# Loading q, k and the weights by GpSimd transfers that cast to f16, with a new order of all steps

## The chip, the cores and the metric

The kernel runs on one core of a Trainium2 chip. Its engines work side by side, each through its own queue in order: TensorE (PE, matmuls; PEld is its weight load), VectorE (DVE), ScalarE (ACT), GpSimd (POOL) and SyncE (SP), which here only issues transfers. 16 DMA engines move the data between HBM and SBUF. The metric is the device time of one launch in microseconds.

## The reference

Sliding-window causal attention (8 batches, 8 heads, 576 positions, head size 64, window 64), and then a gated MLP with a spatial matmul over the positions:

```
scores = q k^T / 8, kept where 0 <= row - column < 64
x      = softmax(scores) v                        # heads side by side: (8, 576, 512)
h      = relu(x @ w_in);  u, v = h[:512], h[512:] # w_in 512 x 1024
v_n    = (v - mean) / sqrt(var + 1e-6)            # over the 512 columns
v_s    = w_spatial @ v_n + b_spatial              # w_spatial 576 x 576
out    = (u * v_s) @ w_out                        # w_out 512 x 512
```

All inputs and the output are float32; the matmuls are in float16.

## The kernel before

The program is a list of small steps. Functions add them to a plan, each with what it computes, the buffers that it takes and uses, and the steps that it depends on. A text at the head of the file, `ORDER`, then gives the order of all steps as words `name:engine:buffers`. The steps are emitted in exactly this order, so it fixes the queue of every engine. Nothing else schedules the program; an instruction waits only where data or a buffer is not ready. `PH` marks a PE step whose matmuls are split into two halves of 64 output rows.

For each batch b and each half g of its heads (four heads) there are these steps:

- `ldk`, `ldq`, `ldv`: loads by SP. k and q come as one transfer of 128 x 1152 f32 each (576 KB) into a staging buffer `nat`, of which there are eight; v comes in five pieces into `natv`. `ldwin`, `ldwsp`, `ldwo`, `ldb` load the weights and the bias through the same `nat` buffers.
- `ck`, `cq`, `cwin`, `cwsp`, `cwo`, `cb`: casts from `nat` to f16, on the engine that `ORDER` names. Those of k and q go into `hqk` (four buffers). `cv` casts v into `hv`; `sl`, `su` and `s4` copy it, shifted by 64 rows, into `hs`.
- `tk`, `tq`: DVE transposes k and q in blocks of 32 x 32, into `qkT`.
- `S` (scores on PE), `E` (exponential on ACT), `M` (the mask, a minimum on DVE), `Z` (row sums on PE), `N` and `n` (the inverse through logarithm and exponential on ACT), `P` (product with v on PE), `X` (multiply by the inverse on DVE). `S_r`, `E_r` and so on do the last 64 rows, for one batch or for a pair of batches.

For each batch follow `V` (the v half of x @ w_in), `Vr` (relu), `Vb` and `Va` (statistics), `L1` and `L2` (the inverse deviation), `A` (normalise), `U` and `Ur` (the u half), `G` (spatial matmul), `Ge` (the gate), `O` (w_out), `Oe` (copy out) and `st` (store). `W` transposes w_spatial on PE, with `We` as its copies. So V of batch 0 needs all X of batch 0 and half of w_in (`ldwin1*`); G of batch 0 needs all A of batch 0 and w_spatial; U needs the other half of w_in.

`D` are dummy matmuls on zeroed scratch data, placed among the first steps; they keep PE busy while it has no data.

The lines that the prediction's rows name: L292, L295, L298, L300 are the copy or cast on ACT, on POOL (k and q in three pieces), on POOL (v) and on any other; L412 and L433 issue the loads of k, q and v; L419 transposes; L479 is S, L489 M, L502 Z, L514 P, L522 X, L606 X_r; L614 and L617 are the whole and the halved matmuls of V, U, G and O; L671 Vb, L728 A, L862 D.

Of the kernel before, what the change touches and what calls it, by code (L numbers as in the profile page):

```python
# [18 lines left out]
D24:PE:0 ldb:DQ:0 D5:PE:1 D21:PE:2 ldk0_0:DQ:1 ck0_0:DVE:0 tk0_0:DVE:0 D18:PE:3 D2:PE:2 D14:PE:2  # L19
D19:PE:3 D10:PE:0 ldq0_0:DQ:2 ldk0_1:DQ:3 ldv0_00:DQ:0 ldq0_1:DQ:4 ldv0_10:DQ:1 D3:PE:3 ldv0_11:DQ  # L20
cv0_10:POOL:0 ldk1_0:DQ:5 ck0_1:ACT:1 ldv0_12:DQ ldv0_13:DQ ldv0_01:DQ cq0_0:DVE:2 ldq1_0:DQ:6
tq0_0:DVE:1 ldv0_02:DQ D1:PE:2 S0_0:PE:0:1 tk0_1:DVE:2 D22:PE:0 E0_01:ACT:0 E0_00:ACT:1 cq0_1:DVE:3
tq0_1:DVE:3 D15:PE:3 D6:PE:1 D0:PE:2 D26:PE:0 D23:PE:3 S0_r:PE:1:0 E0_r0:ACT:0 E0_r1:ACT cv0_11:POOL
sl0_10:DVE:0 M0_00:DVE ldv0_03:DQ su0_10:DVE M0_01:DVE ck1_0:DVE:0 M0_r:DVE D8:PE:1 Z0_00:PE:2
ldv0_04:DQ ldwin110:DQ:7 ldv0_14:DQ ldwin111:DQ ldwin100:DQ:1 S0_1:PE:1:0 N0_00:ACT:0 E0_11:ACT:2
D16:PE:0 D7:PE:3 E0_10:ACT:3 M0_11:DVE Z0_01:PE:1 Z0_r:PE:2 D4:PE:0 Z0_11:PE:3 N0_r:ACT:1
N0_01:ACT:2 cv0_00:ACT:1 N0_11:ACT:3 ldwin101:DQ su0_11:DVE M0_10:DVE D12:PE:0 Z0_10:PE:2 D20:PE:1
sl0_11:POOL tk1_0:DVE:4 sl0_00:ACT:1 N0_10:ACT:4 n0_11:ACT n0_10:ACT cq1_0:POOL:2 tq1_0:DVE:5
ldq1_1:DQ:2 ldk1_1:DQ:3 P0_10:PE:0 P0_11:PE:3 cwin110:ACT n0_01:ACT D11:PE:1 cv0_01:POOL
ldwin000:DQ:4 ldwin010:DQ:5 ldwin001:DQ ldwin011:DQ ldwsp1:DQ:6 X0_10:DVE:0 su0_00:DVE X0_11:DVE  # L30
n0_00:ACT sl0_01:POOL cb:POOL su0_01:POOL S1_0:PE:0:1 D25:PE:2 D13:PE:1 P0_00:PE:0 X0_00:DVE:1
E1_01:ACT:3 s40_1:ACT P0_01:PE:2 D9:PE:3 cwin111:POOL cwin100:POOL cwin101:POOL ck1_1:POOL:1
s40_0:ACT E1_00:ACT:2 cwin010:POOL X0_01:DVE cwin001:POOL cwin011:POOL V0_2:PE:1 M1_01:DVE
Vr0_2:ACT:0 n0_r:ACT P0_r:PE:3 Z1_01:PE:0 V0_0:PE:2 ldwsp3:DQ:0 M1_00:DVE N1_01:ACT:5 Vr0_0:ACT:1
cq1_1:DVE:3 Z1_00:PE:1 V0_3:PH:0 V0_1:PE:2 N1_00:ACT:4 cwin000:ACT Vr0_3:ACT:2 Vr0_1:ACT:3
ldwsp0:DQ:7 ldwsp4:DQ:1 ldwsp2:DQ:2 cwsp1:POOL:6 ldv1_00:DQ:2 ldq2_0:DQ:3 X0_r:DVE:0 tq1_1:DVE:7
Vb0_2:DVE:0 V0_4:PE:3 tk1_1:DVE:8 S1_1:PE:1:0 cwsp3:POOL:0 cwsp0:POOL:1 Vb0_0:DVE:1 Vb0_3:DVE:2
Vr0_4:ACT:4 Va0_3:DVE Vb0_4:DVE:3 Va0_4:DVE Va0_0:DVE Va0_2:DVE Vb0_1:DVE:4 Va0_1:DVE U0_2:PH:1
U0_3:PH:0 ldk2_0:DQ:4 U0_4:PE:2 ldv1_01:DQ ldv1_02:DQ ldv1_03:DQ E1_11:ACT:1 E1_10:ACT:0 cwsp2:POOL
cq2_0:POOL:0 M1_10:DVE ldv1_10:DQ:3 Ur0_2:ACT:0 L10:ACT:0 ldv1_11:DQ ldv1_12:DQ ldv1_13:DQ L20:ACT  # L40
ldv1_14:DQ ldq2_1:DQ:5 ldv1_04:DQ ldk2_1:DQ:6 ldwo00:DQ:0 ldwo01:DQ Ur0_4:ACT:1 S1_r:PE:0:1
Z1_10:PE:3 U0_0:PE:1 ldwo10:DQ:7 ldwo11:DQ U0_1:PE:2 E1_r0:ACT:0 Ur0_3:ACT:2 E1_r1:ACT Ur0_0:ACT:3
# [158 lines left out]
def kernel(  # L201
# [11 lines left out]
    nc = tc.nc  # L213
# [88 lines left out]
    def cost(n, a=True, d=True, p=True, d1=False):  # L302
# [613 lines left out]
```

## Time and profile before

| | |
|---|---|
| time, median of 3 runs | 196.34 us (195.63 to 197.69) |
| profiled execution, first to last instruction | 193.6 us; its own time with what lies around it is not in the profile |
| PE busy | 184.9 us (95%), 3218 matmuls, dummies included |
| DVE, ACT, POOL busy | 163.7 (85%), 157.1 (81%), 87.4 us (45%) |
| DMA moved | 42.73 MB, mean 221 GB/s |
| q and k loads, median to landing | 6.1 and 6.6 us for 576 KB |

PE's busy time counts a matmul up to its modelled end, so a PE that reads as full need not be at its peak, and dummy matmuls count as work. Waits are put down to what ended last. Rows of the timeline give start, duration, engine, line, operation, tiles and count, and in brackets the idle time before them with its releaser.

### The profile page before, as it was taken

The numbers are of one execution on the slowest core, as the hardware profiler recorded it, in microseconds if no ns is written. First come the engines' busy times: TensorE is split into PE (matmuls) and PEld (weight loads), VectorE is DVE, ScalarE is ACT, GpSimd is POOL, SyncE is SP. The second block draws the span as 40 slices with busy tenths as digits, with TensorE's granted clock in tenths as the row PEclk, the third lists the DMA queues.
The fourth block names the chain that finished last, engine by engine and source line by source line (L and its number), as shares of the span: only waits on it lengthen the run. The fifth ranks groups of instructions, "written<-read, shape, count | busy, mean of one in ns | idle before, by whom it ended". The sixth has DMA issues, their size and how long they took to land.

```text
span 193.6 us, 7606 instructions
## 1 busy us (share of the span) xinstructions
PE 184.9 (95%) x3218; PEld 107.0 (55%) x3218; DVE 163.7 (85%) x304; ACT 157.1 (81%) x282; POOL 87.4 (45%) x161
## 2 busy tenths in 40 slices
PE   7798998999999999999999999999999999999991
PEld 2352534556556664656665656565756565665560
DVE  4899899999999999998999999998996967468331
ACT  2269998998999999899979999999999875706430
POOL 4027775849932986701956577615641520000000
PEclk9999999999999999999999999999999999999999
DMA  5999999899989997619987999669958000600445
GB/s 177 373 316 290 391 355 333 168 275 373 242 205 332 261 335 179 149 38 289 367 230 184 310 310 282 196 177 218 306 125 266 22 3 0 224 30 0 135 166 191
DMA packets 50421, 42.73 MB, mean 221 GB/s; under 512 B 39377, under 2 KB 39761, under 8 KB 50386
## 3 DMA queue, kind: packets, MB, share of 16 engines
q1 hardware_dynamic: 50162, 42.04, 73.3%
q8 instruction: 25, 0.41, 0.9%
q10 hardware_dynamic: 224, 0.20, 0.3%
q14 instruction: 10, 0.08, 0.1%
HBM read 32.79 MB, written 9.44 MB: 218 GB/s over the span
## 4 chain that ended last, share of the span: by engine, by line
PE 70%; DVE 13%; ACT 9%; DMA 3%; issue 2%; SPq 1%
PE bank L617 50%; PE bank L614 4%; PE pair L479 4%; PE bank L514 3%; DMA nk<-in_k_dram 3%; PE bank L502 3%; ACT e L486 3%; DVE qT L419 2%; PE bank L702 2%; DVE e L489 2%; DVE kT L419 2%; DVE st L671 2%; DVE g L797 1%; DVE x L522 1%; ACT lz L529 1%
## 5 line engine op out<-in xcount | busy, mean ns | idle before, releaser
L617 PE MATMUL bank<-wspT,vn 128*64 128x512 f16 (+3 forms) x530 | 39.1, 296 | 0.0
L486 ACT ACTIVATE e<-pair 128x1024 f16<-128x1024 f32 x32 | 32.0, 1030 | 1.6 <-PE pair L479 1.4
L797 DVE TENSOR_TENSOR g<-bank,ru 128x512 f16<-128x512 f32 (+1 forms) x36 | 23.3, 654 | 9.4 <-PE bank L617 7.0
L647 ACT COPY ob<-bank 128x512 f32<-128x512 f32 (+1 forms) x38 | 21.9, 591 | 9.7 <-PE bank L617 8.4
L669 ACT ACTIVATE vs<-bank 128x512 f16<-128x512 f32 (+1 forms) x40 | 23.8, 602 | 7.1 <-PE bank L705 5.6
L617 PE MATMUL bank<-x,win 128*64 128x512 f16 (+2 forms) x304 | 29.1, 327 | 0.0
L617 PEld LDWEIGHTS <-vn 128*64 128x64 f16 (+1 forms) x530 | 20.8, 111 | 13.2 <-issue 0.2
L671 DVE BATCH_NORM_STATS2 st<-vs 128x6 f32<-128x512 f16 (+1 forms) x40 | 26.0, 670 | 2.3 <-ACT vs L669 2.2
L298 POOL COPY hs<-hv 64x512 f16<-64x512 f16 (+1 forms) x36 | 20.1, 585 | 16.3 <-ACT hv L292 8.4
L617 PE MATMUL bank<-win,x 128*64 128x512 f16 x216 | 27.0, 379 | 0.0
L617 PE MATMUL bank<-wout,g 128*64 128x512 f16 (+1 forms) x208 | 24.7, 371 | 0.0
L522 DVE TENSOR_TENSOR x<-bank,lz 128x512 f16<-128x512 f32 x32 | 21.2, 684 | 3.5 <-PE bank L514 2.2
L489 DVE TENSOR_TENSOR e<-e,mask 128x1024 f16<-128x1024 f16 x32 | 23.0, 725 | 0.5 <-ACT e L486 0.4
L763 ACT ACTIVATE ru<-bank 128x512 f32<-128x512 f32 (+1 forms) x38 | 21.6, 584 | 1.5 <-PE bank L617 0.8
L295 POOL CAST hk<-nk 128x384 f16<-128x384 f32 x36 | 19.4, 574 | 7.1 <-DMA nk<-in_k_dram 6.7
L529 ACT ACTIVATE lz<-bank 128x512 f32<-128x512 f32 x32 | 19.0, 599 | 1.9 <-PE bank L502 1.6
L298 POOL CAST hv<-nv 128x512 f16<-128x512 f32 x18 | 11.7, 661 | 18.8 <-DMA nv<-in_v_dram 18.7
L419 DVE STREAM_TRANSPOSE kT<-hk 128x576 f32<-128x576 f32 x16 | 19.9, 1241 | 0.2 <-ACT hk L292 0.2
L419 DVE STREAM_TRANSPOSE qT<-hq 128x576 f32<-128x576 f32 x16 | 19.8, 1237 | 0.2
L531 ACT ACTIVATE lz<-lz 128x512 f32<-128x512 f32 x32 | 19.6, 642 | 0.0
L295 POOL CAST hq<-nq 128x384 f16<-128x384 f32 x27 | 14.9, 588 | 10.3 <-DMA nq<-in_q_dram 7.8
L617 PEld LDWEIGHTS <-win 128*64 128x64 f16 x304 | 14.4, 110 | 9.2
(91 smaller groups left out, 298.9 us busy)
## 6 DMA issues: line engine op xcount, KB each, us to landing
nk<-in_k_dram SPq DMA_DIRECT2D x16, 576.0 KB, 6.6
nq<-in_q_dram SPq DMA_DIRECT2D x16, 576.0 KB, 6.1
nv<-in_v_dram SPq DMA_DIRECT2D x64, 128.0 KB, 5.9
out_dram<-ob SPq DMA_DIRECT2D x14, 512.0 KB, 5.8
wi<-in_moe_w_in_dram SPq DMA_DIRECT2D x8, 256.0 KB, 5.8
ws<-in_moe_w_spatial_dram SPq DMA_DIRECT2D x4, 288.0 KB, 7.6
nv<-in_v_dram SPq DMA_DIRECT2D x16, 64.0 KB, 4.5
wo<-in_moe_w_out_dram SPq DMA_DIRECT2D x4, 256.0 KB, 7.2
```

The source lines that it names most:

```text
L295: nc.gpsimd.tensor_copy(o[:, n:n + 384], i[:, n:n + 384])
L298: nc.gpsimd.tensor_copy(o[:, lo:hi, :, :], i[:, lo:hi, :, :])
L419: d = add(f"t{name}{b}_{g}", ("DVE", 1.09), key, lambda e: nc.vector.transpose(qt.t[:, :].rearrange("p (i j) -> p j i", j=18), h.t[:, :].b ...
L486: ex = add(f"E{b}_{g}{u}", ("ACT", 0.91), key, lambda e, u=u: nc.scalar.activation(e2[u].t[:, :, :], sc[u].t[:, :, :], AF.Exp, bias=0.0, s ...
L489: mins.append(add(f"M{b}_{g}{u}", ("DVE", 0.65), key, lambda e, u=u: nc.vector.tensor_tensor(e2[u].t[:, :, :], e2[u].t[:, :, :], mask[:, : ...
L522: lambda e, u=u, ob=ob, lz=lz: nc.vector.tensor_tensor(x.t[:, u, :], ob.t[:, :], lz.t[:, :], ALU.mult),
L617: nc.tensor.matmul(o[c:c + 64, :], w[:, c:c + 64], x, start=start, stop=stop)
L647: lambda e: (nc.vector.tensor_copy if last else nc.scalar.copy)(view(), m.t[rows, 0:n]),
L669: rl = add(f"Vr{b}_{j}", ("ACT", 0.49), key, lambda e: nc.scalar.activation(vs.t[0:jn, :], m.t[0:jn, :], AF.Relu), deps=[pv], acq=[vs], us ...
L671: s1 = add(f"Vb{b}_{j}", ("DVE", 0.6), key + 0.02, lambda e: nc.vector.bn_stats(st6.t[0:jn, 0:6], vs.t[0:jn, :]), deps=[rl], acq=[st6], us ...
L763: lambda e, m=m, ru=ru, n=n: nc.scalar.activation(ru.t[:, 0:n], m.t[:, 0:n], AF.Relu), deps=[pu], acq=[ru], uses=[m])))
L797: nc.vector.tensor_tensor(g.t[:, 0:n], m.t[:, 0:n], ru.t[:, 0:n], ALU.mult)
```

## The change

All transfers of q, k, w_in, w_spatial, w_out and the bias are issued by POOL instead of SP, with an f16 destination, so that they cast on the way. The cast steps `ck`, `cq`, `cwin`, `cwsp`, `cwo` and `cb` and the `nat` buffers go. `hqk` has eight buffers instead of four. Each half of w_in is one transfer, w_out is one, and w_spatial two. The loads of v and the stores stay on SP. The identity for PE's transposes and the two rows of ones move from the start of POOL's queue to a step `consts`. A step `A` may run on POOL, and 22 of the 40 do. A small step `hold` on ACT makes the loads of v of batch 0, half 0, wait for the first k load; it stands behind the first exponential. The dummies are 12 pairs and 31 single matmuls of 512 columns instead of 25 pairs and 18 of 128. `ORDER` is new throughout; of it the first lines before and after stand here.

```diff
 ORDER = """
-D24:PE:0 ldb:DQ:0 D5:PE:1 D21:PE:2 ldk0_0:DQ:1 ck0_0:DVE:0 tk0_0:DVE:0 D18:PE:3 D2:PE:2 D14:PE:2
+D0:PE:0 D1:PE:1 D2:PE:2 D3:PE:3 D4:PE:0 D5:PE:1 D6:PE:2 D7:PE:3 D8:PE:0 D9:PE:1 D10:PE:2 D11:PE:3
+ldv0_10:DQ:0 ldq0_0:POOL:0 tq0_0:DVE:0 ldk0_0:POOL:1 tk0_0:DVE:1 S0_0:PE:0:1 E0_01:ACT:0
...
-NWARM, NFILL, FILL = 27, 2, 9
-BUFS = {"nat": 8, "natv": 4, "hqk": 4, "qkT": 9, ...
+NWARM, NFILL, FILL = 43, 31, 1
+HOLD_AT, HOLD_FOR = 1, (0, 0)
+BUFS = {"natv": 4, "hqk": 8, "qkT": 9, ...
...
-    make_identity(nc, id16[:])
...
-        nc.gpsimd.memset(vn4_t[i][64:65, :], 1.0)
...
+    def emit_consts(e):
+        make_identity(nc, id16[:])
+        for i in range(NSB):
+            nc.gpsimd.memset(vn4_t[i][64:65, :], 1.0)
+    add("consts", ("POOL", 1.8), -2.0, emit_consts)
...
+            ld = add(f"ldwin{half}", ("POOL", 0.85), key + 0.01 * (1 - half),
+                     lambda e, cs=cs: nc.gpsimd.dma_start(
+                         w_in_all[:, :, cs], moe_w_in[:, cs].rearrange("(r p) f -> p r f", r=4)))
...
+        nat = [
+            add("ldwsp0", ("POOL", 0.85), key, lambda e: nc.gpsimd.dma_start(
+                wsp_nat[:, 0:4, :], moe_w_spatial[0:512, :].rearrange("(t p) s -> p t s", t=4))),
+            add("ldwsp4", ("POOL", 0.55), key + 0.001, lambda e: nc.gpsimd.dma_start(
+                wsp_nat[0:64, 4, :], moe_w_spatial[512:576, :]))]
...
-            n = buf("nat", f"n{name}{b}_{g}")
-            ld = add(f"ld{name}{b}_{g}", ("DQ", 0.45), key, lambda e: nc.sync.dma_start(
-                n.t[:, :], src[b, 4 * g:4 * g + 4, :, :].rearrange("h (i j) d -> (h i) (j d)", j=18)),
-                acq=[n], nbytes=1.57, n=128)
             h = buf("hqk", f"h{name}{b}_{g}")
-            c = add(f"c{name}{b}_{g}", cost(1152), key,
-                    lambda e: cp(e, h.t[:, :], n.t[:, :]), deps=[ld], acq=[h], uses=[n])
+            ld = add(f"ld{name}{b}_{g}", ("POOL", 0.55), key, lambda e: nc.gpsimd.dma_start(
+                h.t[:, :], src[b, 4 * g:4 * g + 4, :, :].rearrange("h (i j) d -> (h i) (j d)", j=18)),
+                acq=[h])
...
+        if (b, g) == HOLD_FOR:
+            held, hld = HELD[-1]
+            lds.append(add("hold", ("ACT", 0.1), key, lambda e: nc.scalar.copy(
+                nv.t[0:1, 0, 0, 0:1], held.t[0:1, 0:1]), deps=[hld], acq=[nv], uses=[held]))
...
-            AP.append(add(f"A{b}_{j}", ("DVE", 0.33), key + 0.2, emit_A,
+            AP.append(add(f"A{b}_{j}", [("DVE", 0.33), ("POOL", 0.6)], key + 0.2, emit_A,
```

The start of POOL's queue before, from the end of `keep` on (the first digits in a name are batch and half; the last number only counts):

```order
L247 AFFINE_SELECT keep_79<-keep_79 128x64
masks.py:197 MEMSET id16_83 128x128
masks.py:199 AFFINE_SELECT id16_83<-id16_83 128x128
L264 MEMSET vn4_0_98 1x512
L264 MEMSET vn4_1_99 1x512
L300 CAST hv0_1_154<-nv0_1_149 128x512 x2
L300 COPY hs0_1_279<-hv0_1_154 64x512
L295 CAST hq1_0_408<-nq1_0_165 128x384 x3
L300 CAST hv0_0_385<-nv0_0_145 128x512
```

The same place now:

```order
L243 AFFINE_SELECT keep_79<-keep_79 128x64
L367 DMA hq0_0_132<-in_q_dram 128x1152
L367 DMA hk0_0_136<-in_k_dram 128x1152
L367 DMA hk0_1_199<-in_k_dram 128x1152
L367 DMA hq0_1_207<-in_q_dram 128x1152
L367 DMA hk1_0_309<-in_k_dram 128x1152
L367 DMA hq1_0_315<-in_q_dram 128x1152
L294 COPY hs0_1_350<-hv0_1_242 64x256
L367 DMA hk1_1_439<-in_k_dram 128x1152
L367 DMA hq1_1_509<-in_q_dram 128x1152
L322 DMA win_98<-in_moe_w_in_dram 128x4x512
L329 DMA wspn_100<-in_moe_w_spatial_dram 128x4x576
```

Six loads go out ahead of the first copy, which waits for a cast of v; the rest of the first loads stand behind it.

DVE before, from the first cast on to the transpose of the fourth load:

```order
L300 CAST hk0_0_127<-nk0_0_125 128x1152
L419 STREAM_TRANSPOSE kT0_0_129<-hk0_0_127 128x18x32
L300 CAST hq0_0_163<-nq0_0_141 128x1152
L419 STREAM_TRANSPOSE qT0_0_167<-hq0_0_163 128x18x32
L419 STREAM_TRANSPOSE kT0_1_229<-hk0_1_158 128x18x32
L300 CAST hq0_1_237<-nq0_1_147 128x1152
L419 STREAM_TRANSPOSE qT0_1_239<-hq0_1_237 128x18x32
```

The same place now, up to the first cast of v:

```order
L373 STREAM_TRANSPOSE qT0_0_134<-hq0_0_132 128x18x32
L373 STREAM_TRANSPOSE kT0_0_138<-hk0_0_136 128x18x32
L373 STREAM_TRANSPOSE kT0_1_201<-hk0_1_199 128x18x32
L373 STREAM_TRANSPOSE qT0_1_209<-hq0_1_207 128x18x32
L447 TENSOR_TENSOR e2_0_01_197<-e2_0_01_197,mask_84 128x1024
L294 CAST hv0_1_242<-nv0_1_130 128x512
```

The casts are gone, q comes first, and the transposes follow each other.

DVE before, the last rows ahead of the first V; the X of batch 0 write `x0_0` and `x0_1`:

```order
L300 CAST hk1_0_285<-nk1_0_156 128x1152
L574 TENSOR_TENSOR er_0_275<-er_0_275,mask_88 128x512
L489 TENSOR_TENSOR e2_0_11_359<-e2_0_11_359,mask_88 128x1024
L300 COPY hs0_1_279<-hv0_1_154 64x512
L489 TENSOR_TENSOR e2_0_10_365<-e2_0_10_365,mask_88 128x1024
L419 STREAM_TRANSPOSE kT1_0_400<-hk1_0_285 128x18x32
L419 STREAM_TRANSPOSE qT1_0_412<-hq1_0_408 128x18x32
L522 TENSOR_TENSOR x0_1_461<-bank0_69,lz0_10_404 128x512
L300 COPY hs0_0_402<-hv0_0_385 64x512
L522 TENSOR_TENSOR x0_1_461<-bank3_72,lz0_11_387 128x512
L522 TENSOR_TENSOR x0_0_552<-bank0_69,lz0_00_357 128x512
L522 TENSOR_TENSOR x0_0_552<-bank2_71,lz0_01_383 128x512
```

And now:

```order
L532 TENSOR_TENSOR er_0_238<-er_0_238,mask_84 128x512
L447 TENSOR_TENSOR e2_0_11_320<-e2_0_11_320,mask_84 128x1024
L294 CAST hv0_0_323<-nv0_0_203 128x512
L294 COPY hs0_0_325<-hv0_0_323 64x512 x3
L294 CAST hv0_1_242<-nv0_1_130 128x512
L294 COPY hs0_1_350<-hv0_1_242 64x512 x2
L480 TENSOR_TENSOR x0_0_463<-bank0_69,lz0_00_355 128x512
L373 STREAM_TRANSPOSE kT1_1_504<-hk1_1_439 128x18x32
L480 TENSOR_TENSOR x0_1_506<-bank1_70,lz0_10_341 128x512
L373 STREAM_TRANSPOSE qT1_1_511<-hq1_1_509 128x18x32
L480 TENSOR_TENSOR x0_0_463<-bank3_72,lz0_01_249 128x512
L480 TENSOR_TENSOR x0_1_506<-bank0_69,lz0_11_485 128x512
```

Casts and copies of v, which other engines shared, now stand on DVE here, and the transposes of batch 1, half 1, have moved ahead of the last X.

339 lines of the change are left out of this document (142 added, 197 removed).

## The prediction

> **What bounds the kernel now.** I read the stages first: stretches cut at TensorE's (PE's) first matmul of w_in (23.42 us, step V0_2), its first matmul of w_spatial (38.69, G0_0) and its last matmul (189.37). Columns: length, busy time and count of PE, its weight loads, VectorE (DVE), ScalarE (ACT), GpSimd (POOL), then granted clock, DMA share, GB/s. The last two rows are the same view for the dummy matmuls of line 862 alone.
>
> ```profile
> 0.00:23.42 23.42, 20.05 (x318) 9.29 (x319) 19.34 (x35) 14.17 (x22) 10.91 (x24) 1.00 0.98 307
> 23.42:38.69 15.27, 14.40 (x183) 7.14 (x185) 14.51 (x30) 14.02 (x28) 10.86 (x16) 1.00 0.99 290
> 38.69:189.37 150.68, 150.30 (x2723) 90.53 (x2719) 129.63 (x241) 128.53 (x232) 65.61 (x121) 1.00 0.69 201
> 189.37:193.65 4.28, 0.17 (x4) 0.00 (x0) 0.25 (x1) 0.37 (x1) 0.00 (x0) 1.00 0.56 175
> 0.00:23.42 23.42, 15.48 (x66) 5.43 (x66) 1.00 0.98 307
> 23.42:38.69 15.27, 0.61 (x2) 0.11 (x2) 1.00 0.99 290
> ```
>
> From 38.69 on PE idles 0.38 us in 150.68. Before 23.42 it looks busy, but 15.48 of its 20.05 us are dummies. So I priced every PE step at what its kind takes when nothing holds it; the chain of work that ended last has them (start, us, what):
>
> ```profile
> 59.50 0.60 PE pair L479 x52
> 88.26 0.25 PE bank L514 x12
> 87.18 1.08 PE bank L617 x10
> 92.57 0.22 PE bank L502 x2
> 92.79 1.73 PE bank L617 x16
> ```
>
> A score step S is 0.60, P 0.25, Z 0.22, G 1.08 (ten half matmuls), and V, U and O 0.865 each (16 halves are two steps). All steps together need 164.6 us: 4.0 before 23.42, 13.2 up to 38.69, 147.4 behind. The span of 193.6 is thus 164.6 of work, 19.4 lost before w_in, 2.1 between, 3.3 scattered later, and a tail of 4.3. The change leaves the matmuls alone; **only those 29 us are to be had, and two thirds of them are the start**.
>
> What makes the start long: the timeline's first loads (SP issues), the engines that wait for them, and the DMA rates of two stretches of 5 us.
>
> ```profile
> 1.21 0.38 SPq L412 DMA_DIRECT2D nk<-in_k_dram  x1
> 1.34 0.24 POOL L247 TENSOR_SCALAR_AFFINE_SELECT keep<-keep 128x64 f16<-128x64 f16 x1
> 2.10 0.43 SPq L412 DMA_DIRECT2D nk<-in_k_dram  x1
> 5.26 0.76 DVE L300 CAST hk<-nk 128x1152 f16<-128x1152 f32 x1 [1.66 <-DMA nk<-in_k_dram]
> 8.20 1.15 ACT L292 CAST hk<-nk 128x1152 f16<-128x1152 f32 x1 [6.11 <-DMA nk<-in_k_dram]
> 5.00:10.00 5.00, 3.88 (x69) 1.89 (x68) 4.49 (x5) 1.15 (x1) 0.00 (x0) 1.00 1.09 370
> 10.00:15.00 5.00, 4.91 (x98) 2.62 (x97) 4.86 (x8) 3.40 (x6) 1.53 (x2) 1.00 1.12 316
> ```
>
> The first k lands at 5.26 us, 4.05 after its issue; the third of the 576 KB loads at 8.20. The DMA engines are full from then on, at 370 and 316 GB/s, and DVE works 4.86 of 5 us.
>
> **The change part by part, and the start first.** The casts of k and q leave DVE and ACT, but the loads now start on POOL. Its two selects of `keep` end at 1.58, against SP's first issue at 1.21. No DMA issue of POOL is in the trace: the near rows are SP's issues (0.38 to 0.43) and POOL's own select of a small tile (0.24) and cast (0.57, below); I take 0.8 for one and keep 0.4 and 1.6 as ends. Four issues then end at 4.8. The third load lands at about 8.9 (8.20, plus 0.37 for the start and some of the dearer issues), the fourth a further 1.6 (590 KB at 370 GB/s) and 0.3 of v later: 10.8. Its transpose ends at 12.0. The durations by operation and shape (count, busy, mean ns):
>
> ```profile
> L489 DVE TENSOR_TENSOR e<-e,mask 128x1024 f16<-128x1024 f16 x32 | 23.0, 725 | 0.5 <-ACT e L486 0.4
> L522 DVE TENSOR_TENSOR x<-bank,lz 128x512 f16<-128x512 f32 x32 | 21.2, 684 | 3.5 <-PE bank L514 2.2 <-ACT lz L531 1.1
> L419 DVE STREAM_TRANSPOSE qT<-hq 128x576 f32<-128x576 f32 x16 | 19.8, 1237 | 0.2
> L300 DVE CAST hq<-nq 128x1152 f16<-128x1152 f32 x4 | 3.3, 826 | 0.0
> L574 DVE TENSOR_TENSOR er<-er,mask 128x512 f16<-128x512 f16 x4 | 2.7, 673 | 0.5 <-ACT er L563 0.5
> L300 DVE COPY hs<-hv 64x512 f16<-64x512 f16 x4 | 1.2, 294 | 0.1
> ```
>
> Between that transpose and the last X, DVE now has four masks (2.90), the mask of the remainder (0.67), three casts of v (0.826 scaled from 1152 to 512 elements, 0.37 each, 1.10), five copies into hs (1.47), four transposes (4.96) and four X (2.74): 13.8 us. In the old order v's casts and two transposes were not in this place; three q and k casts went, more came. **V0 therefore starts at 25.9, not at 23.42**, DVE being late. Data: eight loads of q and k, v of batch 0 and half of w_in are 6.95 MB, at 350 GB/s (between 316 and 370) 19.9 us behind 2.1: 22 us, or 25 with v of batch 1 in between, which SP may now issue as soon as v of batch 0 is out. So DMA covers this by 1 to 4 us, no more. At that point S1_1 is done too: 4.6 us of work, 21.3 lost.
>
> The Trainium skill, "DMA: Bandwidth & Descriptors", section "Anatomy of one DMA — SWDGE (gpsimd) path", gives a GpSimd transfer about 2.0 us plus its bytes at 436 GB/s. An estimate by that page: four loads from 1.58 on land by 9.0, V0 starts at 24.1, and the sum below would be 194.2. The trace has no GpSimd load; SP's first one took 4.05 us where the page's form gives 3.4.
>
> **From V0 to G0.** The old stretch, from PE's timeline (brackets: idle before, and its releaser):
>
> ```profile
> 24.02 0.82 PE L614 MATMUL bank<-win,x 128*128 128x512 f16 x3 [0.21 <-DVE x L522]
> ...
> 25.23 1.04 PE L614 MATMUL bank<-win,x 128*128 128x512 f16 x4
> 26.20 0.41 PE L502 MATMUL bank<-e,ones 128*64 128x512 f16 x2
> ...
> 29.85 0.67 PE L479 MATMUL pair<-qT,kT 32*128 32x128 f16 x56 [0.42 <-DVE kT L419]
> 33.41 0.41 PE L502 MATMUL bank<-e,ones 128*64 128x512 f16 x2 [0.24 <-DVE e L489]
> 37.80 0.61 PE L862 MATMUL bank<-scratch 128*128 128x512 f16 x2
> ```
>
> These are 0.21, 0.42 and 0.24 of waits and a dummy of 0.54; the rest of the 2.1 is mostly in unhalved steps, which take up to 0.97 (25.23 to 26.20). The new order has V0 (halved), P0_r, four Z1, V0_4, S1_r, five W and three U here, 10.5 us of work, and S1_1 and its transposes are out. DVE needs four masks, two s4 casts, X0_r, five statistics and their sums, about 8.1, then ACT's two small steps and A0: 35.8. PE is there at 36.4, so DVE is covered by 0.6, less if V0 slips. V0_4 still waits for X0_r; I take 0.9 of waits. G0_1 starts at 37.3. The spatial weights and the other half of w_in (2.4 MB, 6.8 us at 350 GB/s) follow the first half and are needed at about 31 and 33: covered by little.
>
> **The rest.** 149.5 us of matmuls remain. POOL loses these casts:
>
> ```profile
> L295 POOL CAST hk<-nk 128x384 f16<-128x384 f32 x36 | 19.4, 574 | 7.1 <-DMA nk<-in_k_dram 6.7 <-DVE x L522 0.2
> L295 POOL CAST hq<-nq 128x384 f16<-128x384 f32 x27 | 14.9, 588 | 10.3 <-DMA nq<-in_q_dram 7.8 <-DVE e L489 2.3
> L298 POOL CAST hv<-nv 128x512 f16<-128x512 f32 x18 | 11.7, 661 | 18.8 <-DMA nv<-in_v_dram 18.7
> L728 DVE TENSOR_SCALAR vn<-vs,mv,ln 128x512 f16<-128x512 f16 x32 | 12.1, 422 | 2.2 <-ACT ln L718 1.9
> ```
>
> 34.3 us go, with some 9 of weight casts; 38 issues at 0.8 (30 us) and 22 normalisations A come. POOL has none of these now; I price one like its cast of the same shape (0.66), bounds 0.42 (DVE's) and 1.0. POOL stays below its 87 us. DVE loses 22 A (9.3) and six q and k casts (5.2) and gets eight casts of v and ten copies (5.9): 8.6 less of 163.7. ACT loses five q and k casts (5.8) and three of weights. Neither bounds PE; I let a third of the 3.3 of scattered waits go, leaving 2.2, with 0 and 6 as ends, the upper because an issue that waits on POOL now holds back the A's and copies behind it, and G waits for A. The loads of k and q for batch 2 onwards stand 6 us or more of PE work ahead of their transposes in nearly all cases, against 4.05 to land; ldk2_1 is the tightest. At the end A7_1 and A7_4 run on POOL beside three on DVE, 1.3 instead of 2.1 in a row; two PE steps (1.7) hide it, and it costs up to 0.7 if POOL's A takes 1.0.
>
> **Sum.** 37.3 + 149.5 + 2.2 + 4.3 = 193.3, against 193.6. The median of the runs is 196.34, 2.7 above the profiled span; I take that as lying around it. That gives **196.0 us**. A measurement of this kernel tells about 1% (2 us) from no change.
>
> Engines also slow each other: here DVE casts while POOL casts too, and takes 1.17 instead of the 0.76 above.
>
> ```profile
> 14.08 0.92 POOL L300 CAST hv<-nv 128x512 f16<-128x512 f32 x1 [1.97 <-DMA nv<-in_v_dram]
> 14.44 1.17 DVE L300 CAST hk<-nk 128x1152 f16<-128x1152 f32 x1
> ```
>
> With 34 us of POOL casts gone such losses shrink; that is part of why I let waits go. The Trainium skill, "SBUF — State Buffer", section "Who interferes with whom", says the two share a port pair that the first comer holds for its whole instruction, and that loads issued from GpSimd starve when a copy of DVE holds it. By that rule DVE's copies for `mask` at the start would hold POOL's first issues; an estimate by it, two issues held for as long as the cast above took alone (0.76), is 1.5 us, and the sum would be 197.5. The pair above agrees that they collide; no run here shows an issue held.
>
> **Rivals.** *Faster*: an issue costs 0.4 as on SP, the fourth load lands at 9.2, V0 starts at 24.3, and the lighter DVE and ACT leave 0.5 of the waits: 1.6 and 1.7 less, 192.7, between 190.5 and 194.3. For it: DVE is busy for 14.51 of the 15.27 us from V0 to G0, ACT for 14.02, and both lose work in total. Against: DVE has more before V0 than it had.
>
> *Slower by dearer packets*: a casting packet may hold a DMA engine longer than a plain one. The bytes written halve, which is a bound below (half the time); two passes are one above. 5.77 MB of loads before V0 cast, 15.6 us at 370 GB/s. The cover is 1 to 4 us, so from about 1.2 times the price on it decides: at 1.3, 4.7 less 1 of cover, 199.7; at 1.5, 203; at 2, 210. For it: the DMA share is 0.98 and 0.99 up to 38.69.
>
> *Slower by late loads*: POOL takes its queue in order, so an issue behind a copy that waits for v comes late, DVE waits in a transpose, and PE behind it: 1 us for each of three to six such places, 199 to 202. Against it the leads counted above.
>
> *Nothing but a new place*: the casts were hidden, DVE's other work takes their place. That is my forecast.
>
> **How the numbers follow.** Forecast 0.38 (194.4 to 198.3), faster 0.34, dearer packets 0.18, late loads 0.10. The forecast's bounds (V0 from 24.3 to 27.5, waits 0 to 6) spill a little to both sides. 190.5 to 203 leaves out a packet price above 1.5 and the best of the faster case, under 2 in 10. Faster by over 1% 0.35, within 0.37, slower 0.28.
>
> **What would show it.** V0's first matmul at 25.9 with DVE's last X as its releaser, not a DMA; the fourth load's transpose at about 10.8; G0 near 37; PE idle under 1 us behind it. Wrong if V0 waits for w_in, if POOL issues take over 1.6, or if transposes wait for DMA behind 40 us.

## The result, and the profile after

The changed kernel takes 237.5 us (median; 236.2 to 239.6) against 196.6 us (195.6 to 197.7) for the kernel before: 1.210 times as long, 95% interval 1.202 to 1.219. The forecast was 196.0 us with a range of 190.5 to 203, so it was far off. A run that lay over 1.5% above the fastest of its kernel is left out of all times and ratios here. The profiled execution has a span of 236.6 us against 193.6.

First the same stages as in the prediction, cut at TensorE's first matmul of w_in (V0), its first of w_spatial (G0) and its last one. Columns: length, busy time and count of PE, its weight loads, DVE, ACT, POOL, then granted clock, DMA share, GB/s (as bytes written, so a casting load counts half of what it reads).

```profile
0.00:35.77 35.77, 24.18 (x363) 11.29 (x363) 19.40 (x38) 14.28 (x23) 11.78 (x27) 0.81 1.03 182
35.77:46.66 10.89, 10.89 (x107) 5.91 (x106) 9.44 (x24) 10.23 (x22) 2.58 (x2) 1.00 0.70 154
46.66:231.08 184.42, 162.61 (x2830) 94.29 (x2828) 130.63 (x235) 125.20 (x227) 83.41 (x92) 0.94 0.53 120
231.08:236.62 5.54, 0.17 (x4) 0.00 (x0) 0.25 (x1) 0.37 (x1) 0.00 (x0) 0.89 0.42 139
```

V0 starts at 35.77 instead of 23.42, and PE idles 21.8 of the 184.42 us behind G0, where it had idled 0.38 us in 150.68. The granted clock, 1.00 throughout before, is now 0.81 in the start and 0.94 later.

With the prediction's prices of PE's steps (164.7 us in all; the prediction has 164.6) the lost time at any point is the clock time less the priced steps done. At G0 it is 31.0 us (21.5 before), behind it another 35.3 (3.1 before), and the tail is 5.5 (4.3). So **9.5 us went in the start, 32.2 in the batches and 1.2 in the tail**, 43 us in all. Of the 32.2, the G steps hold 24.1 (they ran over their price by 24.8 in total, 0.7 before), P 4.9 and V and O 3.4 together; the rest differs by rounding and small gains.

What PE waited for, after the change: engine and line, what released it, us in total, how often, the longest.

```profile
PE bank L575 <- POOL vn L686: 16.6, 10, 2.6
PE bank L472 <- DVE hs L294: 8.6, 2, 4.5
PE bank L472 <- issue: 3.0, 1, 3.0
PE bank L820 <- DVE scratch L233: 1.3, 1, 1.3
PE bank L572 <- POOL vn L686: 1.2, 1, 1.2
```

L686 is the normalisation A, L472 the step P. The wait for A is 17.8 us in all; the other 7.0 of the 24.8 are G matmuls that take longer than their price. A's own row among the costliest groups (count, busy, mean ns, idle before it):

```profile
L686 POOL TENSOR_SCALAR vn<-vs,mv,ln 128x512 f16<-128x512 f16 (+1 forms) x22 | 48.1, 2191 | 73.5 <-ACT ln L676 50.2
```

One A on GpSimd takes 2.19 us; the prediction had 0.66, with 1.0 as the upper end. How such a wait costs more than itself is seen at batch 1, in PE's timeline and in three stretches of 5 us (columns as above):

```profile
73.86 0.62 PE L575 MATMUL bank<-wspT,vn 128*64 128x512 f16 x4 [1.38 <-POOL vn L686]
76.34 5.33 PE L575 MATMUL bank<-wspT,vn 128*64 128x512 f16 x24 [1.86 <-POOL vn L686]
66.00:71.00 5.00, 5.00 (x80) 2.68 (x76) 4.93 (x11) 4.58 (x12) 3.68 (x5) 1.00 0.70 156
71.00:76.00 5.00, 2.10 (x92) 1.28 (x90) 4.15 (x6) 4.91 (x8) 5.00 (x3) 0.90 0.47 135
76.00:81.00 5.00, 4.66 (x22) 1.97 (x24) 1.98 (x3) 0.08 (x1) 4.76 (x10) 0.50 0.45 66
```

PE waits 3.24 us for two A's, and in the 5 us from 76 on its granted clock is 0.50: the 24 matmuls of 76.34 take 5.33 us, 0.22 each, where a G step of ten takes 1.08, so 24 would take 2.6. These waits thus cost some 2.7 us more behind them.

Now the start. Rows of the timeline: the first and some later loads that GpSimd issues, SP's loads of v once `hold` lets them go, DVE's first and fourth transpose and its last cast of v, and PE's P step.

```profile
1.51 0.74 POOL L367 DMA_DIRECT2D hq<-in_q_dram  x1
6.83 1.26 DVE L373 STREAM_TRANSPOSE qT<-hq 128x576 f32<-128x576 f32 x1 [3.64 <-DMA hq<-in_q_dram]
11.01 1.26 DVE L373 STREAM_TRANSPOSE qT<-hq 128x576 f32<-128x576 f32 x1
11.82 11.63 SPq L391 DMA_DIRECT2D nv<-in_v_dram  x8
14.96 0.77 POOL L322 DMA_DIRECT2D win<-in_moe_w_in_dram  x1
16.99 0.83 POOL L322 DMA_DIRECT2D win<-in_moe_w_in_dram  x1
22.93 0.26 PE L472 MATMUL bank<-e,hs 128*64 128x64 f16 x2 [4.46 <-DVE hs L294]
28.57 0.43 DVE L294 CAST hv<-nv 128x512 f16<-128x512 f32 x1 [5.69 <-DMA nv<-in_v_dram]
```

Up to 12 us it runs as forecast: the fourth transpose ends at 12.27 (forecast 12.0). Then v of batch 0 comes late: `hold` ends at 11.4, SP issues eight of the ten loads of v of batch 0 only from then on, and DVE waits 5.69 us for a piece of v that it casts at 28.57. Between 15 and 25 us the DMA engines were full, and the view by queue says with what (packets, MB written, share of 16 engines):

```profile
q0 software_dynamic: 1069, 1.41, 83.9%
q1 hardware_dynamic: 2077, 0.52, 29.9%
DMA to landing us min/median/max: 3.1/9.1/17.8
```

q0 is GpSimd's queue (k, q, weights), q1 SP's, which carries v alone here. v moves 0.52 MB in 10 us, 52 GB/s; the last row, of the loads of v issued from 12.4 to 35.7 us, has a median of 9.1 us to land and up to 17.8. In the kernel before, all loads stood in one queue, and up to 24 us a load of v landed 4.9 to 7.3 us after its issue.

### The profile page after: what moved, and what is told of

The parts are those of the page before. It is cut to its first block, busy times and chain, and to the rows that moved or that the text cites. A ratio compares the mean times of both kernels' runs of the same rounds, so it can differ in the third digit from the quotient of the medians.

```text
span 236.6 us, 7650 instructions
## 1 busy us (share of the span) xinstructions
PE 197.8 (84%) x3297; PEld 111.5 (47%) x3297; DVE 159.7 (68%) x295; ACT 150.1 (63%) x271; POOL 97.8 (41%) x120
## 4 chain that ended last, share of the span: by engine, by line
PE 43%; POOL 17%; DVE 14%; issue 9%; DMA 8%; ACT 4%; SPq 2%; POOLq 1%; DVEq 0%; ACTq 0%
PE bank L575 33%; POOL vn L686 16%; DMA nv<-in_v_dram 6%; DVE st L629 4%; DMA hk<-in_k_dram 3%; DVE e L447 2%; PE bank L472 2%; PE bank L660 2%; PE pair L437 2%; DVE kT L373 2%; SPq L391 2%; DVE x L480 1%; PE bank L460 1%; PE bank L820 1%; DVE g L755 1%
## 5 line engine op out<-in xcount | busy, mean ns | idle before, releaser
L686 POOL TENSOR_SCALAR vn<-vs,mv,ln 128x512 f16<-128x512 f16 (+1 forms) x22 | 48.1, 2191 | 73.5 <-ACT ln L676 50.2
L575 PE MATMUL bank<-wspT,vn 128*64 128x512 f16 (+3 forms) x530 | 44.7, 315 | 16.7 <-POOL vn L686 16.6
L444 ACT ACTIVATE e<-pair 128x1024 f16<-128x1024 f32 x32 | 31.6, 1024 | 35.9 <-PE pair L437 24.1
L575 PEld LDWEIGHTS <-vn 128*64 128x64 f16 (+1 forms) x530 | 21.2, 115 | 35.7 <-POOL vn L686 21.4
L575 PE MATMUL bank<-x,win 128*64 128x512 f16 (+2 forms) x392 | 33.2, 309 | 0.1
L605 ACT COPY ob<-bank 128x512 f32<-128x512 f32 (+1 forms) x38 | 21.6, 587 | 17.0 <-PE bank L575 13.4
L575 PE MATMUL bank<-wout,g 128*64 128x512 f16 (+1 forms) x264 | 32.3, 381 | 0.0
L575 PE MATMUL bank<-win,x 128*64 128x512 f16 x256 | 32.0, 387 | 0.0
L721 ACT ACTIVATE ru<-bank 128x512 f32<-128x512 f32 (+1 forms) x38 | 21.8, 576 | 9.2 <-PE bank L575 4.9
L447 DVE TENSOR_TENSOR e<-e,mask 128x1024 f16<-128x1024 f16 x32 | 21.7, 692 | 3.3 <-ACT e L444 3.2
L292 POOL COPY hs<-hv 64x512 f16<-64x512 f16 (+1 forms) x26 | 14.1, 572 | 17.9 <-DVE mv L631 11.4
L575 PEld LDWEIGHTS <-win 128*64 128x64 f16 x392 | 16.2, 111 | 10.1 <-issue 0.7
L575 PEld LDWEIGHTS <-x 128*64 128x64 f16 x256 | 15.3, 112 | 11.2 <-issue 0.8
L575 PEld LDWEIGHTS <-g 128*64 128x64 f16 x264 | 15.1, 112 | 11.2 <-issue 0.7
```

The lines of the kernel that those rows point to most:

```text
L444: ex = add(f"E{b}_{g}{u}", ("ACT", 0.91), key, lambda e, u=u: nc.scalar.activation(e2[u].t[:, :, :], sc[u].t[:, :, :], AF.Exp, bias=0.0, s ...
L447: mins.append(add(f"M{b}_{g}{u}", ("DVE", 0.65), key, lambda e, u=u: nc.vector.tensor_tensor(e2[u].t[:, :, :], e2[u].t[:, :, :], mask[:, : ...
L575: nc.tensor.matmul(o[c:c + 64, :], w[:, c:c + 64], x, start=start, stop=stop)
L605: lambda e: (nc.vector.tensor_copy if last else nc.scalar.copy)(view(), m.t[rows, 0:n]),
L686: ENG[e].tensor_scalar(o[0:jn, :], VS[j].t[0:jn, :], mv_t[b % NSB][0:jn, j, 0:1], ln.t[0:jn, 5 + j:6 + j], ALU.subtract, ALU.mult)
L721: lambda e, m=m, ru=ru, n=n: nc.scalar.activation(ru.t[:, 0:n], m.t[:, 0:n], AF.Relu), deps=[pu], acq=[ru], uses=[m])))
```

## The experiments

Each kernel was timed beside the kernel before on the same chip (195.97 to 196.4 us there). The lost time is worked out as above; behind the table each run has its edit, what was expected, and what came. The columns from V0 on are of the profiled execution; that of e2 took 230.7 us, so its lost time is an upper end.

| kernel | us | V0 | G0 | lost by G0 | lost behind | tail |
|---|---|---|---|---|---|---|
| before | 196.6 | 23.42 | 38.69 | 21.5 | 3.1 | 4.3 |
| after | 237.5 | 35.77 | 46.66 | 31.0 | 35.3 | 5.5 |
| e1: after, A on DVE | 221.7 | 35.03 | 45.62 | 30.0 | 19.0 | 5.9 |
| e12: after, v of batch 0 by POOL | 229.7 | 29.77 | 40.61 | 25.0 | 33.2 | 5.0 |
| e8: both | 213.2 | 26.51 | 37.24 | 21.6 | 20.7 | 5.3 |
| e11: e12, A at a copy's price | 204.8 | 26.91 | 37.71 | 22.1 | 10.4 | 5.8 |
| e2: before, A on POOL | 227.6 | 23.94 | 38.99 | 21.8 | 38.1 | 4.4 |
| e5: before, loads alone | 200.0 | 26.95 | 41.63 | 24.4 | 4.6 | 4.2 |

**A on VectorE (e1).** All 22 words of this kind:

```diff
-A0_1:POOL:2
-A0_3:POOL:3
+A0_1:DVE:2
+A0_3:DVE:3
...
```

> The changed kernel with all 40 normalisations A on VectorE, as before the change; nothing else moves. Theory A (the price of A on GpSimd, 2.07 to 2.5 us where 0.66 was assumed, sets most of the loss): the first G steps of each batch no longer wait, the 24 us by which they ran over go, and some of the low clock behind them: 208 to 214 us. Rival Q (the loads that stand in GpSimd's queue in order, and the v loads beside them, set the loss behind the start): the waits move from G to the transposes and P steps, 228 us or more. The start stays as it is in both: V0 near 36, G0 near 46.

Measured 221.7 us, ratio to before 1.126 (1.120 to 1.132): 15.8 us less, and the G steps now run over by 9.0 us instead of 24.8, or by 11.8 with a wait of 2.82 for A that stands ahead of a G step's first matmul and is counted with the step before it. That is between the two theories. PE's waits and, for one G of batch 2, DVE's timeline:

```profile
PE bank L472 <- DVE hs L294: 7.0, 2, 4.6
PE bank L575 <- DVE vn L686: 6.0, 2, 3.1
96.60 1.25 DVE L373 STREAM_TRANSPOSE kT<-hk 128x576 f32<-128x576 f32 x1
97.70 1.24 DVE L373 STREAM_TRANSPOSE qT<-hq 128x576 f32<-128x576 f32 x1
98.78 0.79 DVE L447 TENSOR_TENSOR e<-e,mask 128x1024 f16<-128x1024 f16 x1
99.50 1.96 DVE L686 TENSOR_SCALAR vn<-vs,mv,ln 128x512 f16<-128x512 f16 x4
```

The four A's stand behind two transposes and a mask, an order that made sense while GpSimd was to do them. So A on DVE in this order is not free either, which I hadn't counted.

**The same A's on GpSimd in the kernel before (e2).**

```diff
-            AP.append(add(f"A{b}_{j}", ("DVE", 0.33), key + 0.2, emit_A,
+            AP.append(add(f"A{b}_{j}", [("DVE", 0.33), ("POOL", 0.6)], key + 0.2, emit_A,
```

and the same 22 words of the order set to POOL.

> The kernel before with only one part of the change: the same 22 normalisations A on GpSimd, all loads and casts as before. Theory A: each costs about 2.1 us there, GpSimd also has its casts (87 us of work), and G waits: 20 to 32 us slower than before, 217 to 229. Rival Q: A alone costs little, since the loads do the harm: under 205.

Measured 227.6 us, 1.158 (1.150 to 1.167): theory A, at the upper end. The start is as before (21.8 lost by G0); in the profiled execution of 230.7 us the G steps alone run over by 32.4 us. Rows of its waits and groups:

```profile
PE bank L617 <- POOL vn L728: 14.7, 12, 2.2
L728 POOL TENSOR_SCALAR vn<-vs,mv,ln 128x512 f16<-128x512 f16 x19 | 40.9, 2159 | 43.4 <-ACT ln L718 21.2 <-issue 15.2 <-DMA nv<-in_v_dram 6.9
```

**What makes A dear there (e6).** Six of the 22 in other forms:

```diff
+                if (b, j) in ((0, 3), (2, 2)):
+                    ENG[e].tensor_scalar(o[0:jn, :], VS[j].t[0:jn, :], 0.5, 2.0, ALU.subtract, ALU.mult)
+                elif (b, j) in ((1, 0), (2, 1)):
+                    ENG[e].tensor_scalar(o[0:jn, :], VS[j].t[0:jn, :], ln.t[0:jn, 5 + j:6 + j], None, ALU.mult)
+                elif (b, j) in ((1, 1), (2, 3)):
+                    ENG[e].tensor_copy(o[0:jn, :], VS[j].t[0:jn, :])
```

> The changed kernel, with six of the 22 normalisations on GpSimd in another form, each leaving out part of the computation: two with constants instead of the two scalars per partition, two with a multiplication by one scalar per partition alone, two as plain copies (128x512, f16 to f16 in all). Theory P (the scalars read per partition make A dear on GpSimd): constants near 0.6 us, one scalar near 1.3, the copy near 0.6, the full form 2.07 as before. Rival E (any operation but a copy of this shape is slow there): constants and one scalar both near 2.0, the copy 0.6. The bound of the prediction, 0.42 to 1.0 for the full form, fails in both.

GpSimd's rows that write vn (ns min/median/max, first and last start):

```profile
L693 POOL TENSOR_SCALAR vn<-vs,mv,ln x16: 2065/2074/2510, 43.0 to 207.6; 128x512 f16<-128x512 f16 x13, 64x512 f16<-64x512 f16 x3
L687 POOL TENSOR_SCALAR vn<-vs x2: 1925/1932/1939, 45.4 to 81.8; 128x512 f16<-128x512 f16 x2
L689 POOL TENSOR_SCALAR vn<-vs,ln x2: 1608/1649/1690, 67.9 to 88.9; 128x512 f16<-128x512 f16 x2
L691 POOL COPY vn<-vs x2: 601/664/727, 69.5 to 90.6; 128x512 f16<-128x512 f16 x2
```

Mostly rival E: constants save 0.14 us, one operation instead of two 0.42, and only the plain copy is cheap. The arithmetic is dear, not the scalars read per partition. My price of 0.66 was right for a copy and a third of what the operation takes. The kernel took 225.4 us in its one run.

**Weights issued later (e3, and e4 with A on DVE).**

```diff
-sl0_01:DVE
+ldk1_1:POOL:6 ldq1_1:POOL:7 ldwin1:POOL sl0_01:POOL
...
-ldk1_1:POOL:6
...
-ldq1_1:POOL:7
...
-ldwin1:POOL
...
 ldwsp0:POOL ldwsp4:POOL ldwin0:POOL
```

> The changed kernel, but w_spatial and the second half of w_in are issued behind a GpSimd copy that waits for v of batch 0, while k and q of batch 1 and the first half of w_in are issued ahead of it. Theory S (the v loads of batch 0 on SP's queue are held up because GpSimd issues all weights at once and their packets share the DMA engines): the last v pieces that P0 waits for land by about 24 to 25 instead of 28.5, V0 starts near 32 instead of 35.8, and the whole takes 232 to 235 us. Rival B (only the number of bytes counts, the order of issue doesn't): v as late as before, V0 at 35 to 37, 236 to 239 us.

> Both edits: all A on VectorE, and the late issue of those weights. Theories A and S together: 204 to 210 us, the two gains adding. If the start's gain is taken up by a later wait for the weights (W or U): as the run with A alone, 208 to 214.

e3 took 236.4 us (233.2 to 236.6), e4 219.5. In both the last piece of v was cast at 25.0 instead of 28.6 and 26.6, and V0 moved to 32.90 and 32.91, as theory S had it, but of the 2.9 us that G0 gained over the changed kernel the time of e3 shows 1.1, within its scatter, and e4 is 2.2 us below e1, far from 204 to 210. Read by time, e3 is inconclusive: what still stood beside v (k and q of batch 1, half of w_in) was enough to hold it up, DVE's wait for the piece being 5.37 us in e4.

**No hold on v (e7), and v in GpSimd's own queue (e8).** Both have A on DVE; hold is moved ahead of v of batch 1.

```diff
-hold:ACT:1
...
-ldv0_00:DQ
+ldv0_00:DQ:1
...
-ldv1_10:DQ:2
-ldv0_04:DQ
+ldv0_04:DQ hold:ACT:2 ldv1_10:DQ
```

In e8 the ten loads of v of batch 0 have POOL for DQ, `ENG[e].dma_start` for `nc.sync.dma_start`, and eight of them stand ahead of ldk1_1.

> The changed kernel with all A on VectorE, and v of batch 0 not held back at the start: the step hold stands ahead of v of batch 1 instead, so SP issues all v of batch 0 at once from 0.8 us on. Theory S: v of batch 0 is in by about 15 us, the loads of q and k come up to 3.5 us later, and the wait of P0 for v that lasts till 28.5 goes: V0 at 28 to 30 instead of 34, the whole 214 to 218 (the same kernel with the hold took 221.7). Rival B (bytes alone count): V0 unchanged, 220 to 223.

> As the run before it, but v of batch 0 is loaded by GpSimd's queue, ahead of k and q of batch 1 (plain f32 transfers in the same ten pieces), so that nothing shares the DMA engines with it out of order. Theory S: in one queue the pieces land in the order in which they were issued, v of batch 0 by 18 to 20 us, V0 at 27 to 30, 212 to 217. If a transfer of 512 descriptors is dear to issue on GpSimd (over 1.5 us each), it holds up the rest: V0 after 32, 218 or more.

e7 took 215.7 us with V0 at 29.44, e8 213.2 with V0 at 26.51: theory S in both (V0 of e8 half a microsecond earlier than it had), and the rival of mere bytes falls: up to 26 us the DMA engines wrote 4.5 MB in e1, 4.6 in e7 and 4.7 in e8.

The casts say which of the two edits did it. The last cast of v that P of batch 0 needs starts at 26.59 in e1, at 21.27 in e7 and at 20.16 in e8. So 5.3 us come from leaving out `hold` alone, with v still in SP's queue beside GpSimd's transfers; one queue adds 1.1. V0 itself gains 2.9 us from e7 to e8, more than the last X (1.3), because in e7 S1_1 and the dummies ahead of V0 run at a granted clock of 0.66 (25 to 30 us) and V0 starts 2.1 us behind the last X; in e8 they run at 1.00 and it starts 0.5 behind. Queue and packet were not varied apart in e8: v goes in packets of 256 B in SP's queue and of 4096 B in GpSimd's.

Rows of e8: the price of one load of v on GpSimd, and the start and the next stretch.

```profile
L391 POOL DMA_DIRECT2D nv<-in_v_dram x10 | 7.6, 769 | 1.9 <-DMA hk<-in_k_dram 1.2 <-DMA hq<-in_q_dram 0.7
0.00:26.51 26.51, 20.91 (x365) 10.10 (x365) 20.04 (x38) 14.22 (x22) 19.15 (x37) 1.00 0.97 181
26.51:37.24 10.73, 10.73 (x106) 5.91 (x106) 9.36 (x25) 10.08 (x23) 1.55 (x3) 1.00 1.05 209
```

Without `hold` and with one queue in order, V0 stands at 26.51 and G0 at 37.24. The prediction had 25.9 and 37.3.

**v by GpSimd, A left there (e12).** e8 with the 22 words back on POOL.

> The changed kernel with v of batch 0 on GpSimd's queue and nothing else altered: the 22 normalisations are on GpSimd in full. It is the fourth corner beside the changed kernel (237.5), the one with A on VectorE (221.7) and the one with both (213.2). If the two terms add: 8 to 10 us less than the changed kernel, 227 to 230, V0 near 26.5, G0 near 38 and the waits at G as they were. If A on GpSimd takes up what the start gains: 233 or more.

Measured 229.7 us, 1.170 (1.166 to 1.174): the gains of the two edits are 15.8 and 7.8 us, together 23.6, and both at once gave 24.3. They add. The profiled execution had V0 at 29.77 and G0 at 40.61, some 3 us later than expected, so it shows only 6.0 of the start's 9.4: its last X ended at 27.7 (e8: 26.0), and V0 came 2.0 us behind it, again behind dummies at a clock of 0.66.

**A at the price that I had assumed (e9, e11).** e12 with the 22 A's on GpSimd as copies (the subtraction and the scaling left out); in e11 each copy waits for the statistics:

```diff
+if e == "POOL":
+    nc.gpsimd.tensor_copy(o[0:jn, 0:1], ln.t[0:jn, 5 + j:6 + j])   # e11 only
+    nc.gpsimd.tensor_copy(o[0:jn, :], VS[j].t[0:jn, :])
```

> The changed kernel with v of batch 0 on GpSimd's queue, as in the run e8, and the 22 normalisations on GpSimd again, but as plain copies of the same shape (the subtraction and the scaling are left out of those 22), so that one takes about the 0.66 us that the prediction had assumed. Theory T (the two terms that failed, v behind GpSimd's transfers and the price of A on GpSimd, hold nearly all of the 43 us lost): V0 near 26.5, G0 near 37.2, at most 6 us lost behind it, 195 to 200 us. Rival N (the new order itself loses time in the batches, in late loads or a late VectorE): 205 us or more.

> As the run e9 (v of batch 0 on GpSimd's queue, the 22 normalisations there as plain copies, so that the subtraction and the scaling are left out), but each copy follows a copy of one column of ln, and so waits for the statistics as a real A does. In e9 the copies ran before the statistics were done, so its 202.25 us is a bound from below. Theory T (with A at the assumed price and v in one queue the prediction's sum nearly holds): 201 to 206 us, G0 near 37.5, at most 11 us lost behind it. Rival D (the wait for the statistics, not the price, is what A on GpSimd costs): the G steps wait again, 208 or more.

e9 took 202.3 us, between its two theories; its copies ran ahead of the statistics, which made it too kind. e11 took 204.8 us, 1.043 (1.039 to 1.048), within theory T, and rival D falls: the G steps run over by 0.6 us in all. Its rows: the copy, and the three stages.

```profile
L688 POOL COPY vn<-vs 128x512 f16<-128x512 f16 x19 | 12.8, 673 | 1.2
0.00:26.91 26.91, 21.62 (x364) 10.37 (x365) 20.02 (x38) 14.33 (x22) 19.16 (x37) 1.00 0.95 174
26.91:37.71 10.80, 10.80 (x106) 5.91 (x106) 9.43 (x24) 10.15 (x23) 2.41 (x5) 1.00 1.10 217
37.71:197.30 159.59, 154.53 (x2830) 95.94 (x2828) 130.51 (x235) 125.18 (x227) 56.95 (x111) 0.99 0.65 146
```

From e12 to e11 the time falls by 24.9 us: that is what the price of A was worth, the lower clock behind its waits included.

**The loads alone (e5, e10).** The order of before, with each load of q, k and the weights as a GpSimd casting transfer where SP had issued it:

```diff
-ldk0_0:DQ:1 ck0_0:DVE:0 tk0_0:DVE:0
+ldk0_0:POOL:0 tk0_0:DVE:0
...
-ldwin110:DQ:7
+ldwin1:POOL
...
-cwin110:ACT
```

> One part of the change alone: q, k and all weights loaded by casting GpSimd transfers (in the places where SP issued them), the casts and the f32 staging gone, but every other step in the order of before, and all A on VectorE. Theory S (the v loads on SP's queue share the DMA engines with GpSimd's transfers and get some 50 GB/s of them, so the start gets longer; the new order and A on GpSimd do the rest of the harm): V0 between 26 and 31 us instead of 23.4, nearly nothing lost behind it, 197 to 204 us. Rival Q (loads that stand in GpSimd's queue behind copies come late in every batch): 5 us or more lost behind G0, 205 to 215. Were casting loads a gain by themselves: under 194.

Measured 199.96 us, 1.020 (1.016 to 1.025): slower, by just about 2%, and in theory S's range. Its stages:

```profile
0.00:26.95 26.95, 22.49 (x319) 9.91 (x319) 16.18 (x31) 13.85 (x22) 15.97 (x34) 1.00 1.01 180
26.95:41.63 14.68, 14.33 (x183) 7.20 (x185) 12.40 (x28) 12.20 (x25) 1.82 (x3) 1.00 1.18 202
41.63:193.81 152.18, 150.40 (x2723) 90.69 (x2718) 127.52 (x241) 124.48 (x227) 49.66 (x85) 1.00 0.66 148
```

Behind G0 nothing much is lost (4.6 us), though 34 us of GpSimd's casts are gone: they had been hidden, and loads in GpSimd's queue did not come late. The start is 3.5 us longer. The profile has both v later there (10.9 us from issue to landing in the median of the loads up to V0, 6.9 before) and q (PE waits 2.86 us for its first transpose, 1.12 before); which of them makes the start longer was not separated.

e10 is e5 with the loads of v of batch 0 on POOL too, between k and q, and hold ahead of v of batch 1:

```diff
-ldv0_00:DQ:0
+ldv0_00:POOL:0
...
-ldv1_00:DQ:2
+hold:ACT:2 ldv1_00:DQ
```

> As the run with the loads alone (old order, all A on VectorE), but v of batch 0 is loaded by GpSimd's queue too, between k and q in the order in which SP had issued them, and v of batch 1 waits for ScalarE's first copies of V0. Theory S: the start is again one queue in order, VectorE has 3 casts fewer, V0 at 23 to 25 us instead of 26.95, 194 to 198 us. If GpSimd's issues (16 more at about 0.75) now make its own casts of v late: V0 at 26 or later, 199 to 203.

e10 took 206.2 us and missed the times of both. V0 stood at 26.20, where the second theory had it; but the hold that I put ahead of v of batch 1 let those loads start at 31.95 only, and the next load of q, which takes the buffer that the hold reads, stood in GpSimd's queue behind it for 7.2 us, so P1 came late. The kernel tests its own hold and not the queue.

No version is faster than the kernel before.

## Why the prediction was wrong, step by step

- **What bounds the kernel** stands: 29 us were to be had, two thirds of them in the start, and e5 shows that the casts in the batches were hidden. But what can be lost has no such bound, and I spent the working on the small side.
- **Issues and the first four loads** were right: issues took 0.54 to 0.83 us (0.8 taken), and the fourth transpose ended at 12.27 (12.0).
- **"So DMA covers this by 1 to 4 us, no more"** failed. I added up 6.95 MB as if it landed in the order of need. But `hold`, to which I gave no term, let eight of the ten loads of v of batch 0 out from 11.4 us only; v stood in SP's queue, everything else in GpSimd's, and GpSimd issued all of w_in and w_spatial within 3 us from 14.96 on. Late issue beside these transfers made v late: without `hold` the last cast of v comes 5.3 us earlier (e7), with one queue 1.1 more (e8). In e8 the same sum held to 0.6 us at V0 and 0.1 at G0; that it came so near is in part luck, since e12, with the same loads, was 3.9 off at V0. The term was 9.5 us, and I had a rival neither for it nor for its place: my "late loads" were loads held back in GpSimd's queue; these were loads held back in SP's and then beside it. The Trainium skill, "DMA: Bandwidth & Descriptors", section "Queues, rings and completion order", says that each DMA engine goes round its queues packet by packet. The rows by queue agree: both progressed from 15 to 25 us, the small packets of v at 52 GB/s. I had used that page for its fixed cost and not for this.
- **A at "0.66, bounds 0.42 (DVE's) and 1.0"** failed, and it is the largest term: 22 at 2.19 us, worth 24.9 us between e12 and e11. The price was drawn from a cast, which moves data and computes nothing, and the upper end of 1.0 stood on no row. POOL's total, which I put below 87 us, came to 97.8, still under half of the span: the cost is latency ahead of G, two to four A's in a row with PE waiting. The Trainium skill, "GPSIMD Engine Reference", section "4.1 Engine selection", calls operations with one input roughly line-rate there; here that holds for the copy (0.66 us beside 0.42 for VectorE's A) and not for this operation, which takes five times VectorE's.
- **"Leaving 2.2, with 0 and 6 as ends"** was too low: e11, free of both terms, still loses 10.4 us behind G0, 5.3 of it counted with P steps. The longest wait there is not for v: it lasts 2.99 us up to 123.49, in the middle of a P step, and the profile names no engine and no load that ended it ("issue"). The DMA records have a packet of 16 KB in the instruction queue (q8) that ended at 122.06, 1.4 us before PE went on. The changed kernel's wait of 2.96 us up to 147.15 ends 1.3 us behind such a packet, and so do, by 1.2 to 1.6 us, all 15 waits of PE over 0.15 us that the fourteen profiles put down to "issue". So PE most likely waited for its own instructions; no run tried it.
- **The tail**, taken as 4.3, is 5.5: ScalarE's last copy now waits for VectorE's.
- **The rivals.** Dearer packets: the first load took 5.3 us from its issue at 1.51 to the transpose at 6.83, SP's first 4.05, and the fourth came as forecast. The DMA records settle it: a packet of k or q took 192 ns in the median (2304 B written), 178 ns before (4608 B), 1.08 times, below the 1.2 from which the rival counted. The two sentences from the Trainium skill did not hold either: its form gives 3.4 us for that first load, and GpSimd's issues were not held up by VectorE's copies for mask (0.74 us the first, 0.54 and more the others).
- **What would have shown it** did not: V0 did not wait for w_in, no issue took over 1.6 us, no transpose waited for DMA behind 40 us. The list named only what I had thought of.
- **"The median is 2.7 above the profiled span; I take that as lying around it"** was 1.0 too much: the run that was profiled after the change took 238.3 us for a span of 236.6, so 1.7 lie around it.

What stays open: 8.8 us between e11 and before (9.5 in the profiled spans), of which the profiles give 0.6 to the start, 7.3 to the batches and 1.5 to the tail, without a run for each. How much of the loss is the lower clock behind the waits was seen at batch 1 and in front of V0 but not separated by a run.

## What to carry to other kernels

An operation that moves to an engine on which the trace doesn't show it has no bound from a copy of the same shape; where it stands on the path to the bounding engine, multiply by several and see whether the forecast's sign still holds. Bytes divided by bandwidth say when data lands only if it is issued in the order of need; when a change holds a load back or splits the loads over two queues, ask which small transfers now run beside which large ones. An order of work made for one place of an operation doesn't fit another: with A back on VectorE the new order lost 20.7 us behind G0 (e8), the old one 4.6 (e5).

## What the runs showed of the hardware

- On GpSimd a 128x512 f16 subtract and multiply took 2.07 to 2.5 us, one operation 1.65, a copy 0.66; 64 rows took as long as 128 (2.16 and 2.20 us on average).
- v in 256-byte packets on SP's queue, most of them issued from 11.4 us on, moved at 52 GB/s beside GpSimd's transfers; without `hold` a load still took up to 13.9 us to land (e7; up to 7.3 before), but the last was cast 5.3 us earlier; in GpSimd's own queue (e8) a load of v cost 0.77 us to issue, and the last cast came 1.1 us earlier still.
- A casting packet of k or q took 192 ns, a plain one 178 ns.
- Waits of 3.2 us in TensorE's work, with four matmuls between them, were followed by 5 us at a granted clock of 0.50.
- Each of 15 waits of TensorE that have no releaser in the profile ended 1.2 to 1.6 us behind a packet of 16 KB in an instruction queue.
